# A recurrence's transposed decay products emitted ahead of the update's copy, its diagonal behind the routing, and a new order of the last steps

## The chip, the cores and the metric

One core of one Trainium2 chip. The time is device microseconds (us) of one execution of the whole program. The engines are TensorE (PE; its weight loads are listed as PEld), VectorE (DVE), ScalarE (ACT), GpSimd (POOL) and SyncE (SP, which issues most of the transfers).

## The reference, cut to what matters

Three stages follow each other. First a recurrence over 768 positions, for 4 batches and 8 heads with 48 channels:

```python
for t in range(S):
    kt, vt, rt = (k[:, :, t], v[:, :, t], r[:, :, t])
    cur = np.einsum('bhd,bhe->bhde', u[None] * kt, vt)
    y[:, :, t] = np.einsum('bhd,bhde->bhe', rt, state + cur)
    state = w[None, :, :, None] * state + np.einsum('bhd,bhe->bhde', kt, vt)
```

Then each of the 3072 tokens (384 channels) with a positive skip score goes to the one of 8 experts with the largest logit, `y = gate * relu(x @ w1[e]) @ w2[e]`, and is added to its input. Then a soft mixture: 32 slots, each a softmax-weighted sum over all tokens, go through 8 experts, and every token takes a softmax-weighted sum of the slots' results.

## The kernel before, in words

The sequence is cut into 6 chunks of 128 positions; with 4 batches that gives 24 tiles, and the recurrence is a loop (line 1012) of 24 steps `i`, one tile each, chunk after chunk. The order of the work is written out by hand: inside `manual_schedule` (line 489) each engine executes its instructions in the order in which the program emits them, and the framework only adds the waits that the tiles' reads and writes call for. Where two instructions for different engines stand in the program so decides nothing about their engines' own order, but does decide which waits for which when they touch the same tile.

A step `i` does, by helper:

- `scores(i)` (line 637): TensorE forms the masked products of r and k in PSUM tile `sc`; `later` copies one part of it out on ScalarE (line 702). Then come the two products of the tile before, `inter(i-1)` (the state's share, line 728) and `av(i-1, 0)` (first half of the scores times v, line 747), and after these the optional `between()`. Then a PSUM tile `ud` of one bank is taken (line 653). It has three column ranges: 0 to 127 for the decay products `dt_` (line 657) and, later, for their transpose `dtk`; 32 columns `rp` for the routing's places; 192 columns `up` for the update of the state. ScalarE copies `dt_` to SBUF as `dts` (line 659).
- `trx(i-2)` (line 754) transposes the finished output of two tiles before into `x`, with a ScalarE copy (line 759).
- `prep(i+1)` forms r and k scaled by the decays on VectorE (lines 626, 627) and a product on GpSimd (line 629); `prepk` a further one on GpSimd.
- `upd(i)` (line 670, steps 0 to 19) writes the update into `up`; `moved(i)` (line 686) copies it out on ScalarE; `bonus(i)` (line 673) transposes `dts` into `dtk` on TensorE. In the program `moved` stands ahead of `bonus`.
- `av(i-1, 1)` is the second half of the products of the tile before; its result is copied to `yt` by ScalarE (line 752).
- `past(i)` (line 696) masks the scores into `at` on VectorE, and `amask(i)` (line 708) overwrites their diagonal from `dtk`. `av(i, 0)` of the next step needs both.

Among these lie parts of the routing for groups of four tiles, one part in each step from 5 on. With `i - 5 = 4 rc + rb`: at rb 1 (steps 6, 10, 14, 18) `route1` forms the logits on TensorE; at rb 2 (7, 11, 15, 19; called routing steps below) `route2` transposes them, ScalarE copies them (line 855) and `route2b` finds the expert in eight small VectorE instructions (lines 870 to 889); at rb 3 (8, 12, 16, 20; placing steps below) `route3` writes the places into the `rp` columns of `ud` on TensorE, and VectorE works out the gates and places (`weave`, lines 913 to 927, of which line 924 reads `rp`) and the counts (937, 938); at rb 0 `route4` (lines 945, 946). `hots` (line 792) makes a one-hot row of 256 columns per tile. All this VectorE work is emitted behind `amask` of its step. The last 8 tiles form groups 4 (16 to 19), 5 (20, 21) and 6 (22, 23), which are routed in steps 21 to 23 and in the tail behind the loop (line 1125).

The tail finishes tiles 22 and 23, routes groups 5 and 6 (`direct` forms group 6's logits in PSUM, line 845), stores x, and forms the list `idg` of token numbers per expert: products at lines 1153 and 809, cast at line 1166. Between these TensorE also does the first third of a weighted sum over the tokens (`w1g.some(6)`, line 128). With `idg` GpSimd gathers the tokens (line 1189), and the expert stage starts (lines 1254 on); from there on TensorE is busy nearly throughout.

Of the kernel before, what the change touches and what calls it, by code (L numbers as in the profile page):

```python
# [8 lines left out]
F32 = mybir.dt.float32  # L9
# [10 lines left out]
P = 128  # L20
# [3 lines left out]
E = 8  # L24
# [447 lines left out]
def tile_main(ctx, tc, rk, kv, wu, wcat, phi, w1, w2, v1, v2, r_in, k_in, v_in, w_in, u_in, wcn, out, dbg=None, force=False):  # L472
# [199 lines left out]
    def bonus(j):  # L672
        nc.tensor.transpose(T[j]["dtk"], T[j]["dts"], ident)  # L673
# [8 lines left out]
    def moved(j):  # L682
        t = T[j]
        if j < NT - B:
            t["us"] = sp[j][1] if j < B else wk.tile([PR, 4, D], F32, tag="us", name=f"us{j}")
            nc.scalar.copy(t["us"], t["up"])
# [7 lines left out]
    def past(j):  # L694
        t = T[j]
        nc.vector.tensor_mul(t["at"][:, :, 0:4], t["sc"][:, :, 0:4], mh.rearrange("s (a o t) -> s a o t", a=1, o=1).to_broadcast([P, 2, 4, HT]))
        t["past"] = True

# [5 lines left out]
    def amask(j):  # L704
        t = T[j]
        if "past" not in t:
            past(j)
        nc.vector.copy_predicated(  # L708
            t["at"][:, :, 0:4],
            ih_i.rearrange("s (a o t) -> s a o t", a=1, o=1).to_broadcast([P, 2, 4, HT]),  # L710
            t["dtk"].rearrange("s (p o r) -> s r p o", o=1, r=32)[:, 0:2].to_broadcast([P, 2, 4, HT]),
        )
# [89 lines left out]
    def stored(j0, nb):  # L802
        nc.sync.dma_start(out=x_d.rearrange("(p j) n -> p j n", j=NT)[:, j0 : j0 + nb], in_=x[:, j0 : j0 + nb, 0:DM])
# [7 lines left out]
    lx = mk.tile([P, 4, 32], F32, name="lx")  # L811
    mcs = mk.tile([P, 5], F32, name="mcs")

    GR = [(4 * c, 4) for c in range(NC_ - 1)] + [(20, 2), (22, 2)]
# [196 lines left out]
    if True:  # L1011
        for i in range(NT):
# [4 lines left out]
            if i == 0:  # L1017
                prep(0)
                for hf in range(2):
                    r0 = 64 * hf  # L1020
                    nc.vector.tensor_copy(usel[r0 : r0 + D, :, hf : hf + 1], wt[r0 : r0 + D, 1, :].rearrange("p (a o) -> p a o", o=1))
            scores(i, lambda: route1(5) if i == 23 else None)
            if i > 1:
                trx(i - 2)
            if i == 21:
                route1(4)
            if rok and rb == 3 or i == 22:
# [5 lines left out]
            if i == 23:  # L1033
                past(23)
                mrt = ps.tile([P, 1, 32], F32, tag="t", name="mrpt")
                nc.tensor.matmul(mrt.rearrange("p o s -> p (o s)"), onesf[0:32], dgt, start=True, stop=True)
                nc.scalar.copy(lx[:, 0:1, :], mrt)
                nc.gpsimd.tensor_sub(ltm[:, 0:16, :], ltm[:, 0:16, :], lx[:, 0:1, :].to_broadcast([P, 16, 32]))
                route2(5)
# [17 lines left out]
            if i == 22:  # L1057
                c4pt = ps.tile([P, P], F32, tag="r", name="c4pt")
                nc.tensor.transpose(c4pt, c4t.rearrange("p q s -> p (q s)"), ident)
            moved(i)  # L1060
            bonus(i)
            if i > 0:
                av(i - 1, 1)
            if i in (13, 17, 21, 22):
                gathered(len(LI))
            past(i) if i < 23 else None
            if i == 22:
                nc.vector.tensor_reduce(mcs[:, 0:1], c4pt, axis=AX.X, op=ALU.max)
                dgt = rt.tile([32, 32], F32, tag="dg", bufs=1, name="dgt")
                nc.vector.tensor_scalar(dgt, ident[0:32, 0:32], mcs[0:32, 0:1], None, op0=ALU.mult)  # L1070
            amask(i)
            if i == 22:
# [4 lines left out]
            if i == 21:  # L1077
                nc.vector.tensor_reduce(cmax, cmg.rearrange("t g s -> t s g"), axis=AX.X, op=ALU.max)
                c4t = fourfold(nc, "t", rt, cmax)
                route2b(4)  # L1080
            elif rb == 0 and 1 <= rc < 4:
                route4(rc - 1)
            if rok and rb == 2 and rc < 4:
                route2b(rc)
            if rok and rb == 3:
                weave("gpgpg", g=gates(rc), p=places(rc))
                count(rc)
                tokens(rc, nc.gpsimd)
                hots(rc, (0,) if rc < 3 else (0, 1), nc.vector)
                if rc == 3:  # L1090
                    route4(3)
# [9 lines left out]
            if i % B and 9 <= i < 22:  # L1101
                hots(i // B - 2, (i % B,) if i < 20 else (2, 3), nc.vector)
            if i % B == 1 and 9 <= i < 25:
# [17 lines left out]
            if i == 6:  # L1121
                sf = rt.tile([P, E], F32, tag="sf", bufs=1, name="sf")
                nc.vector.tensor_reduce(sf, ident.rearrange("p (q r s) -> p s q r", q=4, s=E)[:, :, :, 0:2], axis=AX.XY, op=ALU.add)
                nc.vector.tensor_copy(selb, sf)
        stored(20, 2)
        inter(23)
        route2b(5)
        nc.scalar.activation(ltm[:, 0:16, :], ltm[:, 0:16, :], AF.Exp)
        av(23, 0)
        fz = T[23]["rp"][:, 3 * E : 4 * E]  # L1130
        nc.tensor.matmul(fz, ones, eb2, start=True, stop=True)
# [5 lines left out]
        hots(5, range(2), nc.gpsimd)  # L1137
        direct(6, 0)
        nc.tensor.matmul(fz, ones, fs, start=True, stop=True)
        av(23, 1)  # L1140
        scst.close()
        qst = ExitStack()
        pr = qst.enter_context(tc.tile_pool(name="pr", bufs=1, space=PSUM, side="right"))
        pc = Banks(tp=[(pr, "tp", 2)], ds=[(pr, "ds", 1)])
        trx(23, "tp", pc)
        stored(23, 1)
        direct(6, 1)
        trx(22)
        stored(22, 1)
        idp = ps.tile([P, 2, E], F32, tag="r", name="idp")  # L1150
# [507 lines left out]
```

## Time and profile before

| what | value |
|---|---|
| time, median of 3 runs | 360.18 us (360.09 to 366.7) |
| the profiled execution's own time | 361.89 us |
| its span, first to last instruction | 360.1 us |
| TensorE, busy share of the span | 91% |
| VectorE | 62% |
| ScalarE | 44% |
| GpSimd | 38% |
| mean granted TensorE clock | 0.979 of full speed |

A timeline's row is: start in us from the span's start, duration in us, engine, line, operation, output <- inputs, shapes, count; in brackets how long the engine had been idle before it and what ended that. Several equal instructions in a row are merged into one. A row of waits is: engine, tile and line that waited, what it waited for, us in total, times, the longest. Times inside the profile are those of the profiled execution; the part of its 361.89 us outside the span is 1.79 us.

### The profile page before, as it was taken

To read this page: it belongs to the slowest core of one execution; us is meant where nothing else is said; L and a number is where in the kernel's file an instruction comes from. 1 tells how busy PE (TensorE), PEld (TensorE's weight loads), DVE (VectorE), ACT (ScalarE), POOL (GpSimd) and SP (SyncE) were. 2 spreads that over 40 slices of the span, in tenths; PEclk is the share of its full clock that TensorE was granted. 3 is DMA by queue.
4 is the path that set the end of the run, shared out by engine and by line. 5 is a ranking of instruction groups with operands and counts; after the bars stand their busy time and mean duration, and the time that the engine had idled before them with its cause. 6 is when DMAs were issued, how large, how long until landed. Compare 5 with 4: busy or idle time off the path is not lost. (4 is left out here: it accounts for less than half of the span.)

```text
span 360.1 us, 10416 instructions
## 1 busy us (share of the span) xinstructions
PE 328.3 (91%) x4316; PEld 263.2 (73%) x4316; DVE 222.1 (62%) x514; ACT 160.2 (44%) x351; POOL 138.4 (38%) x175
## 2 busy tenths in 40 slices
PE   8888889888898889899999999999999999999860
PEld 3556676676767565599999999998899999733350
DVE  6455578584867853668576657567476765416660
ACT  2234444444444535246465556464465652311270
POOL 3837666575744161850525252432225202020000
PEclk9999999999999996999999999999999999999995
DMA  7975568476677962689778796978975549669586
GB/s 209 271 204 165 178 181 271 145 257 188 183 213 260 386 226 76 186 295 329 250 268 274 251 308 208 305 247 286 320 227 157 181 153 291 239 198 371 180 314 220
DMA packets 45751, 85.29 MB, mean 237 GB/s; under 512 B 3854, under 2 KB 26688, under 8 KB 45696
## 3 DMA queue, kind: packets, MB, share of 16 engines
q1 hardware_dynamic: 43040, 80.63, 68.1%
q0 software_dynamic: 2128, 3.74, 3.9%
q8 instruction: 36, 0.59, 0.7%
q10 hardware_dynamic: 528, 0.16, 0.2%
q14 instruction: 19, 0.16, 0.1%
HBM read 74.49 MB, written 10.10 MB: 235 GB/s over the span
## 5 line engine op out<-in xcount | busy, mean ns | idle before, releaser
L1254 PE MATMUL hp<-xhl,wa 128*128 128x256 f32 x192 | 48.5, 289 | 0.2 <-ACT xhl L1244 0.2
L1255 PE MATMUL hp<-xhl,wa 128*128 128x256 f32 x192 | 47.1, 282 | 0.0
L1279 PE MATMUL yp<-wb,hh 128*128 128x384 f32 x128 | 45.1, 352 | 0.0
L992 DVE TENSOR_TENSOR wa<-w,wa 128x768 fp32r<-128x768 f32 x32 | 30.5, 956 | 22.0 <-ACT wa L1004 22.0
L1281 PE MATMUL yp<-wb,hlo 128*128 128x384 f32 x128 | 42.9, 335 | 0.0
L1280 PE MATMUL yp<-wb,hh 128*128 128x384 f32 x128 | 42.9, 335 | 0.0
L629 POOL TENSOR_TENSOR pd<-rkb 112x512 f32<-112x512 f32 x24 | 30.6, 1275 | 31.2 <-PE ud L657 22.8
L708 DVE COPY_PREDICATED at<-ih,ud 128x512 f32<-128x512 int32 x24 | 17.7, 740 | 39.9 <-PE ud L673 39.6
L1189 POOL DMA_INDIRECT xg<-x_d,idg x16 | 19.2, 1202 | 53.6 <-DVE x L1287 39.4
L1309 POOL DMA_INDIRECT lt_d<-lsr,ids x16 | 17.7, 1107 | 52.4 <-ACT xhl L1244 29.8
L1254 PEld LDWEIGHTS hp<-xhl,wa 128*128 128x128 f32 x192 | 36.4, 189 | 0.5 <-ACT xhl L1244 0.5
L1255 PEld LDWEIGHTS hp<-xhl,wa 128*128 128x128 f32 x192 | 36.4, 190 | 0.0
L992 DVE TENSOR_TENSOR wb<-w,wb 128x768 fp32r<-128x768 f32 x32 | 30.5, 954 | 2.4 <-ACT wb L1004 2.3
L1264 ACT ACTIVATE hh<-hp 128x512 fp32r<-128x512 f32 x32 | 19.1, 598 | 26.0 <-PE hp L1257 26.0
L1004 ACT CAST wb<-w 128x768 fp32r<-128x768 f32 x32 | 26.8, 837 | 8.8 <-PE yp L1281 5.0
L1265 DVE SCALAR_TENSOR_TENSOR hlo<-hp,hh 128x512 fp32r<-128x512 f32 x32 | 22.0, 687 | 12.4 <-ACT hh L1264 12.4
L1257 PE MATMUL hp<-xhl,wa 128*128 128x256 f32 x192 | 28.2, 283 | 0.0
L1004 ACT CAST wa<-w 128x768 fp32r<-128x768 f32 x32 | 26.9, 840 | 0.0
L1279 PEld LDWEIGHTS yp<-wb,hh 128*128 128x128 f32 x128 | 24.1, 188 | 3.5 <-issue 3.5
L747 PE MATMUL yp<-at,kvt 64*48 64x64 f32 (+3 forms) x800 | 26.0, 245 | 0.2
L1257 PEld LDWEIGHTS hp<-xhl,wa 128*128 128x128 f32 x192 | 25.3, 192 | 0.0
L747 PEld LDWEIGHTS yp<-at,kvt 64*48 64x48 f32 (+1 forms) x800 | 20.9, 121 | 5.3 <-PE wp L498 2.2
(344 smaller groups left out, 686.0 us busy)
## 6 DMA issues: line engine op xcount, KB each, us to landing
w<-in_w_dram SPq DMA_DIRECT2D x32, 768.0 KB, 5.5
v<-in_v_dram SPq DMA_DIRECT2D x29, 768.0 KB, 6.4
rkb<-in_rk_dram SPq DMA_DIRECT2D x24, 448.0 KB, 5.2
kvt<-in_kv_dram SPq DMA_DIRECT2D x24, 384.0 KB, 3.9
x_d<-x SPq DMA_DIRECT2D x5, 768.0 KB, 8.7
out_dram<-ob SPq DMA_DIRECT2D x5, 768.0 KB, 6.1
x<-in_v_dram SPq DMA_DIRECT2D x2, 768.0 KB, 5.9
ltt<-in_v_dram SPq DMA_DIRECT2D x1, 768.0 KB, 7.2
```

Source lines behind the costliest of these rows:

```text
L629: nc.gpsimd.tensor_mul(t["pd"], rkt[:, 0], rkt[:, 1])
L747: nc.tensor.matmul(d, kvt[s0 : s0 + HT, 1, h * D : h * D + m], w, start=(c == ph == z == 0), stop=(ph == z == 1))
L992: nc.vector.tensor_sub(lv, sl, hv.bitcast(F32))
L1004: nc.scalar.copy(hv, sl)
L1189: nc.gpsimd.indirect_dma_start(out=o, out_offset=None, in_=src, in_offset=bass.IndirectOffsetOnAxis(ap=idg[:, bl, e : e + 1], axis=0), bou ...
L1254: nc.tensor.matmul(hp[:, f, :], hi[:, k, fs], xh[:, k, :], start=(k == 0 and f == 0), stop=False)
L1255: nc.tensor.matmul(hp[:, f, :], lo[:, k, fs], xh[:, k, :], start=False, stop=False)
L1257: nc.tensor.matmul(hp[:, f, :], hi[:, k, fs], xl[:, k, :], start=False, stop=(k == 2 and f == 1))
L1265: nc.vector.scalar_tensor_tensor(hlo, hp, 0.0, hh.bitcast(F32), op0=ALU.max, op1=ALU.subtract)
L1279: nc.tensor.matmul(YP[e][bl], hh[:, f, bs], hi[:, f, :], start=st, stop=False)
L1280: nc.tensor.matmul(YP[e][bl], hh[:, f, bs], lo[:, f, :], start=False, stop=False)
L1281: nc.tensor.matmul(YP[e][bl], hlo[:, f, bs], hi[:, f, :], start=False, stop=en)
```

## The change

- `bonus(i)` is emitted ahead of `moved(i)` instead of behind it.
- `amask(i)` is emitted at the end of its step, behind the routing's VectorE instructions; in step 21 behind the column maximum and ahead of `route2b(4)`. `past` is emitted at its one place in every step, 23 too.
- `hots` for group 3 (two tiles in step 20, two in step 21) go to GpSimd instead of VectorE.
- In steps 21 and 23 `route1` stands ahead of the decay products and of `trx`; in step 23 the row of maxima (`topped`: a product, a ScalarE copy, a GpSimd subtraction) stands ahead of `route1(5)` instead of behind `trx(21)`.
- In the tail the sum `fz` gets a PSUM tile of its own, tag `y`, instead of columns of `ud`; `trx(22)` moves to right behind `route3(5)`; `direct(6, 0)` goes behind `av(23, 1)`; the exponential over the first 16 tiles goes behind `trx(23)`; tiles 22 and 23 are stored in one transfer.

```diff
     def past(j):
...
-        t["past"] = True
...
     def amask(j):
         t = T[j]
-        if "past" not in t:
-            past(j)
...
+    def topped():
+        mrt = ps.tile([P, 1, 32], F32, tag="t", name="mrpt")
+        nc.tensor.matmul(mrt.rearrange("p o s -> p (o s)"), onesf[0:32], dgt, start=True, stop=True)
+        nc.scalar.copy(lx[:, 0:1, :], mrt)
+        nc.gpsimd.tensor_sub(ltm[:, 0:16, :], ltm[:, 0:16, :], lx[:, 0:1, :].to_broadcast([P, 16, 32]))
...
-            scores(i, lambda: route1(5) if i == 23 else None)
+            scores(i, lambda: (i == 23 and topped(), route1(i // 2 - 6)) if i in (21, 23) else None)
             if i > 1:
                 trx(i - 2)
-            if i == 21:
-                route1(4)
...
             if i == 23:
-                past(23)
-                mrt = ps.tile([P, 1, 32], F32, tag="t", name="mrpt")
...
                 route2(5)
...
+            bonus(i)
             moved(i)
-            bonus(i)
             if i > 0:
                 av(i - 1, 1)
...
-            past(i) if i < 23 else None
+            past(i)
...
-            amask(i)
             if i == 22:
                 weave("pgpgg", g=gates(4), p=places(4))
...
                 c4t = fourfold(nc, "t", rt, cmax)
+                amask(21)
                 route2b(4)
...
-                hots(rc, (0,) if rc < 3 else (0, 1), nc.vector)
+                hots(rc, (0,) if rc < 3 else (0, 1), nc.vector if rc < 3 else nc.gpsimd)
...
-                hots(i // B - 2, (i % B,) if i < 20 else (2, 3), nc.vector)
+                hots(i // B - 2, (i % B,) if i < 20 else (2, 3), nc.vector if i < 20 else nc.gpsimd)
...
+            if i != 21:
+                amask(i)
         stored(20, 2)
         inter(23)
         route2b(5)
-        nc.scalar.activation(ltm[:, 0:16, :], ltm[:, 0:16, :], AF.Exp)
         av(23, 0)
-        fz = T[23]["rp"][:, 3 * E : 4 * E]
+        fz = ps.tile([P, E], F32, tag="y", name="fz")
         nc.tensor.matmul(fz, ones, eb2, start=True, stop=True)
...
-        direct(6, 0)
+        trx(22)
         nc.tensor.matmul(fz, ones, fs, start=True, stop=True)
         av(23, 1)
+        direct(6, 0)
...
         trx(23, "tp", pc)
-        stored(23, 1)
+        stored(22, 2)
+        nc.scalar.activation(ltm[:, 0:16, :], ltm[:, 0:16, :], AF.Exp)
         direct(6, 1)
-        trx(22)
-        stored(22, 1)
```

## Rows read from the trace of the kernel before

**Rows 1.** Waits of TensorE, 0 to 150 us: the two largest of line 673.

```profile
PE ud L673 <- ACT us L686: 7.6, 16, 0.5
PE ud L673 <- ACT sp L686: 1.7, 4, 0.4
```

**Rows 2.** Timeline of step 15, a routing step.

```profile
88.58 0.54 PEld L670 LDWEIGHTS ud<-kvt,kt 128*64 128x64 f32 x16 [0.17 <-issue]
...
88.69 0.30 ACT L855 COPY lg<-lgp 128x168 f32<-128x168 f32 x1
...
...
89.72 0.14 PEld L673 LDWEIGHTS ud<-ident,dts 128*128 128x128 f32 x1 [0.60 <-ACT us L686]
89.73 0.33 PE L673 MATMUL ud<-ident,dts 128*128 128x128 f32 x1 [0.48 <-ACT us L686]
...
90.09 0.74 DVE L708 COPY_PREDICATED at<-ih,ud 128x512 f32<-128x512 int32 x1 [2.16 <-PE ud L673]
...
90.72 0.31 DVE L870 TENSOR_TENSOR lg<-lg,lgp 128x168 f32<-128x168 f32 x1
...
91.61 0.47 PEld L747 LDWEIGHTS yp<-at,kvt 64*48 64x48 f32 x16
...
92.77 0.68 DVE L626 TENSOR_TENSOR rks<-rkb,prt 112x512 f32<-112x512 f32 x1
```

**Rows 3.** Timeline of step 1: a product and a copy of other columns of its tile.

```profile
16.31 0.27 ACT L659 COPY dts<-ud 128x128 f32<-128x128 f32 x1 [1.35 <-PE ud L657]
...
16.67 0.64 PE L670 MATMUL ud<-kvt,kt 128*64 128x48 f32 x16 [0.43 <-issue]
```

**Rows 4.** Timeline of step 16, a placing step.

```profile
93.26 0.54 PEld L670 LDWEIGHTS ud<-kvt,kt 128*64 128x64 f32 x16
...
95.49 0.18 DVE L924 TENSOR_TENSOR r<-ud,oh 128x32 f32<-128x32 f32 x1
...
96.29 0.48 PEld L747 LDWEIGHTS yp<-at,kvt 64*48 64x48 f32 x16
...
96.64 0.68 DVE L626 TENSOR_TENSOR rks<-rkb,prt 112x512 f32<-112x512 f32 x1
```

**Rows 5.** Timeline of step 8, the first placing step.

```profile
54.73 0.18 DVE L924 TENSOR_TENSOR r<-ud,oh 128x32 f32<-128x32 f32 x1
...
56.33 0.68 DVE L626 TENSOR_TENSOR rks<-rkb,prt 112x512 f32<-112x512 f32 x1
```

**Rows 6.** Timeline of steps 21 to 23.

```profile
123.63 0.65 DVE L792 TENSOR_SCALAR hot<-ipl,sl 128x256 bf16<-128x256 f32 x2
...
127.57 3.66 POOL L792 TENSOR_SCALAR hot<-ipl,sl 128x256 bf16<-128x256 f32 x4 [3.44 <-DVE se L915]
...
130.27 0.40 PE L1036 MATMUL mrpt<-dgt,onesf 32*128 32x32 f32 x2 [0.57 <-ACT x L759]
```

**Rows 7.** Timeline of the tail.

```profile
133.46 0.17 PE L899 MATMUL ud<-eb,ones 128*128 128x16 bf16 x1 [0.82 <-ACT fs L1133]
...
135.92 0.60 PE L758 MATMUL trp<-ident,yt 112*128 112x112 f32 x4 [0.71 <-ACT yt L752]
...
137.77 0.17 DVE L875 TENSOR_REDUCE mx<-lgp 128x2 f32<-128x16 f32 x1 [3.02 <-PE lgp L845]
...
139.55 2.78 PE L128 MATMUL dpst<-x,ltt 128*32 128x385 f32 x12
...
142.26 0.29 PEld L809 LDWEIGHTS <-hot 128*128 128x128 bf16 x8 [1.24 <-issue]
...
144.76 1.48 PE L128 MATMUL dpst<-x,ltt 128*32 128x385 f32 x10
```

**Rows 8.** Busy time by stretch: us; PE, PEld, DVE, ACT, POOL; granted clock; DMA share; GB/s.

```profile
136.00:138.00 2.00, 2.00 (x15) 2.00 (x16) 0.23 (x3) 0.48 (x1) 0.27 (x1) 0.70 0.01 5
...
140.00:142.00 2.00, 2.00 (x12) 0.37 (x4) 0.69 (x4) 2.00 (x3) 0.00 (x0) 0.50 0.31 97
142.00:144.00 2.00, 2.00 (x19) 0.78 (x18) 1.20 (x4) 0.19 (x1) 0.17 (x1) 0.59 0.50 121
```

More of the change, by code (lines that the diff above doesn't have):

```diff
@@ L1033, in tile_main @@
             if i == 23:
-                past(23)
-                mrt = ps.tile([P, 1, 32], F32, tag="t", name="mrpt")
-                nc.tensor.matmul(mrt.rearrange("p o s -> p (o s)"), onesf[0:32], dgt, start=True, stop=True)
-                nc.scalar.copy(lx[:, 0:1, :], mrt)
-                nc.gpsimd.tensor_sub(ltm[:, 0:16, :], ltm[:, 0:16, :], lx[:, 0:1, :].to_broadcast([P, 16, 32]))
                 route2(5)
```

## The prediction

> **What bounds the kernel now.** I read the page first: by the table TensorE is busy for 91% of the span and no other engine above 62%. So a change pays by the idle time that it takes from TensorE, or by work that it takes off the path where TensorE waits. The second view is TensorE's list of waits over the recurrence and the tail [rows 1]. One line leads it: the transposition of the decay products, L673, waits 20 times for the copy of the update, L686, once in each of steps 0 to 19 and 9.3 us in all. The reader is to see in the timeline of one step [rows 2] why. The last weight load of the update ends at 88.58 + 0.54 = 89.12, and TensorE loads nothing until 89.72, when the copy is done: 0.60 us in which its weight path stands still. The transposition reads none of what the copy reads (`dts` lies in SBUF) and writes other columns of `ud`. That the wait is kept by tile and not by columns is seen in step 1 too: the update starts at 16.67 when the copy of the decay products, 16.31 + 0.27 = 16.58, is out of its way, though it writes other columns [rows 3]. The third view is VectorE's place in the step: the diagonal's instruction, L708, waits 2.16 us idle for the transposition, and the routing's work stands behind it [rows 2]. The last view is the tail up to the list of tokens, where TensorE waits at several places [rows 7] and has half its clock for a stretch [rows 8].
>
> **The order of transposition and copy.** With the transposition first in the program, TensorE has no wait left between update and transposition: the transposition needs only `dts`, long copied. Its weight load then starts at 89.12 or a little later. From above the gain is the 0.60 of the weight path, from below the 0.48 that the matmul's own row shows [rows 2]; nothing excludes a few hundredths lost at the hand-over, so I take 0.56, and 0.51 for the first four steps, whose matmul rows are 0.05 shorter (1.7 / 4 against 7.6 / 16 [rows 1]). The copy in turn now waits for the transposition. It starts some 0.37 later against the update's end, but has room: ScalarE's next copy, that of the second products, comes behind these products anyway, and GpSimd needs the update a chunk later. What is late next? `av(i, 0)` of the next step, if the diagonal isn't ready.
>
> **The diagonal behind the routing.** In a step with little routing VectorE does that work in the 2 us in which it waited, and the diagonal follows the transposition as before; that hides it. In two kinds of steps it doesn't.
>
> Routing steps (7, 11, 15, 19), by step 15 [rows 2]: the copied logits are there at 88.69 + 0.30 = 88.99, the eight instructions and the one-hot row take from 90.72 to the next instruction's start at 92.77, so 2.05. The diagonal would start at 88.99 + 0.03 + 2.05 = 91.07 (0.03 is the hand-over as it was before L708: 90.09 less 90.06) and be ready at 91.07 + 0.74 + 0.03 = 91.84. Before, the products' load began at 91.61. So this step loses 0.23 instead of gaining 0.56. Step 7 has no one-hot row (92.77 - 92.51 = 0.26) and comes out at -0.03, about nothing.
>
> Placing steps (8, 12, 16, 20), by step 16 [rows 4]: L924 reads the places in `ud`. By the rule of rows 3 it now waits for the transposition, which is emitted ahead of it and writes that tile. The update's load comes at 93.26 + 0.23, its end 0.54 later at 94.03; the diagonal used to start 0.37 behind the transposition's load (90.09 - 89.72 [rows 2]), so L924 starts at 94.40. From there to the next VectorE instruction were 96.64 - 95.49 = 1.15; the diagonal starts at 95.55, and the products at 95.55 + 0.77 = 96.32 against 96.29 before. The pair 15 and 16 costs 0.03 and gains nothing, 11 and 12 the same. In step 8 the chain is 56.33 - 54.73 = 1.60 long [rows 5], 0.45 more, and the pair 7 and 8 costs 0.03 - 0.26 + 0.45 = 0.22.
>
> The Trainium skill, PSUM — Partial Sum Buffer, section on bank collisions, says that two engines must be kept apart by bank and quadrant of partitions and not by address. Rows 3 agree, and it speaks against this part. If columns counted, L924 would not wait, the placing steps would each gain some 0.5, and the whole would be 1.6 us better; by the rule it is as worked out above.
>
> So of steps 0 to 18, thirteen gain in full: 4 x 0.51 + 9 x 0.56 = 7.08. Less 0.22 + 0.03 + 0.03 that is 6.8 us at the start of step 19.
>
> **The last steps and the tail.** I look for what can leave TensorE's path up to the list of tokens. Two one-hot rows on VectorE, 0.65 [rows 6], go to GpSimd, where one takes 3.66 / 4 = 0.92 and the engine had been idle for 3.44: hidden, as their reader is a step away. The wait of the product of maxima, 0.57 [rows 6], goes, since it no longer stands behind the copy of a transposed tile. In the tail the wait for `fs`, 0.82, goes as the sum gets its own bank; the wait for the last copy of yt, 0.71, is filled with `direct(6, 0)`; and one set of transpositions, 0.60 by the row of its twin, moves from the stretch behind into one where TensorE waited [rows 7]. All five make 3.35, the upper end. Against it stand step 19 (0.23) and step 20, whose diagonal comes behind weave, counts and `route4`: about 0.5, between nothing and the 0.60 that a routing step's swing less its own gain can reach. That leaves 2.6. The lower end counts the tail's two waits alone, 0.82 + 0.71, less those 0.7: 0.8. I take 2.6, since VectorE's chain is what the removed waits ended in. Stores and gather: the x of tiles 22 and 23 now leaves in one transfer on SP's queue, behind the copy of the later; both copies are earlier than before, and the gather still waits for the list. The exponential moves behind that copy on ScalarE and is read only by the weighted sum, some microseconds on.
>
> The sum is 6.8 + 2.6 = 9.4 us. The expert stage behind is bound by TensorE and moves as a whole. The sum is made in a span of 360.1 us, 361.89 with the 1.79 around it; the median of the runs is 360.18, so the time would be 350.8 us.
>
> **The clock.** TensorE's clock was at half (1.2 GHz) from inside the stretch 136 to 138 to inside 142 to 144: 0.6 x 2 + 4 + 0.82 x 2 = 6.8 us [rows 8], behind the tail's idle time. The weighted sum took 0.23 per product in that stretch (2.78 / 12) and 0.15 at full clock (1.48 / 10) [rows 7]. I assume that the fall comes again about there, since the new tail still waits for group 5's experts and then does only small products.
>
> **The rivals.**
> - *The clock holds.* Less idle time stands ahead of the place of the fall. Then the first twelve products take 1.4 us less (139.55 to 142.26 is 2.7, half of it), and the list comes that much sooner: 360.18 - 10.8 = 349.4. For it: two of the waits ahead go. Against: the small products stay.
> - *The diagonal comes later than worked out.* If readers of `ud` on two engines are also kept apart, L924 waits for the copy of the update as well, some 0.35 more in each of steps 8, 12 and 16, and if the transposition's gain is only the 0.48 of its row, thirteen steps lose 0.08 more: 1.05 + 1.0. With 2 us for the tail instead of 2.6 that is 6.7, so 353.5. For it: VectorE has no slack in the pairs. Against: nothing in the rows shows such a wait.
> - *The transposition still waits.* If its wait came from something else than the order in the program, the 7.08 are gone and the diagonals are late for nothing: some 0.8 us in each of three pairs. Against that stand the tail's 2.6: 360. Against it: the wait ends with that copy in 20 of 20 steps.
> - *Slower: the clock falls inside the recurrence.* New waits of TensorE for the diagonal come in groups: steps 7 and 8, 11 and 12, 15 and 16, 19 and 20, and 22. If the clock fell there as in the tail, each fall would cost half of 6.8, or 3.4 us. Three falls eat the gain (10.2 of 9.4), and five make it 360.18 - 9.4 + 17 = 367.8. Against it: every step had an idle 0.6 before with the mean clock at 0.979, and the new waits are no longer than those that go. The Trainium skill, TensorE: Matmul & The Clock Gate, section on oscillation, says that idle gaps between bursts of matmuls throttle the engine again; the half clock behind the tail's waits agrees, and no row shows it in the recurrence.
>
> **How the numbers follow.** Forecast 350.8: 0.45 (own range 349.3 to 352.3). Clock holds, 349.4: 0.25. Diagonal late, 353.5: 0.21. Transposition still waits, 360: 0.06. Clock falls, 367.8: 0.03. A measurement of this kernel can tell about 2% from no change, so faster is below 353.0: nearly all of the first two and a third of the third, held back a little as my durations come from one execution: 0.73. Slower, above 367.4: 0.03. Within: 0.24. The range runs from 347.0, where the tail gives its whole 3.35 (0.75 more), the 0.60 is reached in each of thirteen steps (0.7) and the clock holds, with 1 us over for what the rows of one execution leave open, to 354.5, which takes in the late diagonal and a tail with 1 us less.
>
> **What would show it.** Right: L673 has no wait for L686 in the list of waits, and 20 steps' L673 load follows L670's at once; L686 now waits for L673. L747 waits for L708 by 0.5 to 1 us in steps 7, 8, 11, 12, 15, 16, 19 and 20, and in no other up to there. L924 starts right behind the transposition. Step 19 starts some 6.8 us earlier, the list (L1166) some 9.4. The prediction is wrong if waits for L708 show in steps with little routing, if L673 waits for another engine, if the stretch from step 19 to the list isn't some 2.6 us shorter, or if the granted clock is below 1.00 between 10 and 130 us.

## The result, and the profile after

The changed kernel takes 356.97 us (median of 20 runs, 353.27 to 362.22); the kernel before, run beside it on the same chip, takes 361.85 (20 runs). The ratio is 0.985, with an interval of 0.982 to 0.987: a gain of 1.5%, within the 2%. The forecast was a gain of 9.4 us; about half of it came. A median is of all executions; a ratio and its interval leave out those more than 1.5% above the fastest of their kernel. The granted clock differs between executions of one program (0.964 to 0.987 here) and the time mostly goes with it, 353.27 us at 0.987 and 356.98 at 0.976. The rows below are of one execution each, that of the changed kernel one of 355.71 us at 0.985; those of e4_swap_only, e5_wok_late and e9_mixed, further down, took 364.11, 361.53 and 355.44 us, more than these kernels' medians.

The page's table and clock of the changed kernel:

```profile
span 354.0 us, 10396 instructions
## 1 busy us (share of the span) xinstructions
PE 326.0 (92%) x4316; PEld 261.7 (74%) x4316; DVE 230.9 (65%) x510; ACT 160.8 (45%) x351; POOL 141.7 (40%) x179
...
PEclk9999999999999999999999999999999999999985
```

VectorE's share of the span is up from 62% (222.1 us), though it executes four instructions fewer. TensorE's waits, 0 to 150 us, answer to [rows 1]:

```profile
PE yp L744 <- DVE at L705: 6.8, 9, 1.4
...
PE ud L910 <- DVE oh L892: 0.4, 1, 0.4
```

The 9.3 us of L673 are gone from the list; the products (L744, before L747) wait for VectorE's diagonal (L705, before L708) instead, nine times, 6.8 us. VectorE's own waits in the same stretch, first the diagonal of the kernel before, then the changed kernel:

```profile
DVE at L708 <- PE ud L673: 39.6, 20, 3.6
```

```profile
DVE at L705 <- ACT us L686: 8.7, 5, 2.1
DVE at L705 <- ACT sp L686: 8.0, 4, 3.0
DVE at L705 <- PE ud L673: 4.1, 2, 2.5
...
DVE r L927 <- ACT us L686: 3.4, 3, 1.1
```

The reader is to see the name L686: before, the diagonal waited 20 times for the transposition; now it waits for that twice and nine times for the copy of the update, which only reads the same tile. The places' product (L927, before L924) waits for that copy too. The third reading is the timeline of steps 11 and 12, a routing and a placing step, which answer to [rows 2] and [rows 4] (L789 is the one-hot row, before L792):

```profile
66.52 0.33 DVE L873 TENSOR_TENSOR lg<-lg,lgp 128x168 f32<-128x168 f32 x1 [0.94 <-ACT lg L858]
...
68.22 0.19 DVE L892 SCALAR_TENSOR_TENSOR oh<-lgp,m 128x32 bf16<-128x32 f32 x1
...
68.33 0.70 DVE L789 TENSOR_SCALAR hot<-ipl,sl 128x256 bf16<-128x256 f32 x1
68.35 0.52 POOL L680 TENSOR_TENSOR tmp<-sp,pt 112x192 f32<-112x192 f32 x1
...
68.95 0.71 DVE L705 COPY_PREDICATED at<-ih,ud 128x512 f32<-128x512 int32 x1
...
69.71 0.55 PE L744 MATMUL yp<-at,kvt 64*48 64x128 f32 x16 [0.85 <-DVE at L705]
...
71.88 0.33 PE L673 MATMUL ud<-ident,dts 128*128 128x128 f32 x1
...
72.30 0.32 ACT L686 COPY us<-ud 112x192 f32<-112x192 f32 x1 [0.63 <-PE ud L673]
...
72.65 0.19 DVE L927 TENSOR_TENSOR r<-ud,oh 128x32 f32<-128x32 f32 x1 [1.13 <-ACT us L686]
...
73.52 0.70 DVE L789 TENSOR_SCALAR hot<-ipl,sl 128x256 bf16<-128x256 f32 x1
73.55 0.52 POOL L680 TENSOR_TENSOR tmp<-sp,pt 112x192 f32<-112x192 f32 x1
...
74.14 0.71 DVE L705 COPY_PREDICATED at<-ih,ud 128x512 f32<-128x512 int32 x1
...
74.90 0.55 PE L744 MATMUL yp<-at,kvt 64*48 64x128 f32 x16 [0.84 <-DVE at L705]
```

Two things stand here that the forecast did not have (the first was a rival's). The places' product starts when the copy of the update ends (72.30 + 0.32 = 72.62), not behind the transposition. And the one-hot row takes 0.70 where it took about 0.34, and is done (0.70 on from 73.52 is 74.22) soon after the GpSimd multiply that began beside it (74.07). Between 50 and 103 us there are eleven such rows, each 0.69 us or longer, and each ends 0.15 or 0.16 us behind the end of a GpSimd instruction. VectorE's one-hot rows by form, 0 to 135 us, first of the changed kernel, then of the kernel before, with busy us and mean ns of one:

```profile
L789 DVE TENSOR_SCALAR hot<-ipl,sl 128x256 bf16<-128x256 f32 x14 | 10.4, 748 | 0.0
```

```profile
L792 DVE TENSOR_SCALAR hot<-ipl,sl 128x256 bf16<-128x256 f32 x16 | 5.4, 345 | 0.0
```

It is the same instruction at more than twice the time. The worst case of this kind is in step 4, where constants are made; first the cast of the kernel before, then the timeline of VectorE and GpSimd in the changed kernel:

```profile
35.04 0.21 DVE L1114 CAST tf<-tj_i 128x48 f32<-128x48 int32 x1
```

```profile
30.38 1.27 POOL L629 TENSOR_TENSOR pd<-rkb 112x512 f32<-112x512 f32 x1 [0.58 <-PE ud L657]
...
30.70 1.96 DVE L1110 CAST tf<-tj_i 128x48 f32<-128x48 int32 x1
...
31.61 1.00 POOL L635 TENSOR_TENSOR kt<-kvt,pktok 128x384 f32<-128x384 f32 x1
...
33.60 0.71 DVE L705 COPY_PREDICATED at<-ih,ud 128x512 f32<-128x512 int32 x1
```

A cast of 48 elements per partition, 0.21 us before, lasts until both GpSimd instructions are over (32.61), and step 5 is 0.55 us longer than before.

The time from the start of one step's scores to the next, taken from the timelines (all in us; the last column sums steps 3 to 18). The products that need the diagonal of a step belong to the next one, so a late diagonal in step 4 shows in step 5, one in steps 7 and 8 in 8 and 9:

```
                  step 5   8+9   12+13   16+17   19 to 22   3 to 18
before             4.44   9.16    9.60    9.49      20.31     81.56
after              4.99  10.15   10.53   10.53      18.67     80.51
e1_front           4.06  10.93    8.80    8.82      20.17     81.19
e2_copy_first      4.52  10.24   10.53   10.52      18.69     84.68
e4_swap_only       4.07  10.92    8.80    8.81      23.98     80.54
e6_fill_behind     4.06   8.98    9.31    9.31      18.58     76.17
e7_wok_psum        4.06   8.95    8.81    8.80      20.17     75.76
e8_own_bank        4.03   8.10    9.27    9.26      21.06     75.40
e11_hots_behind    4.99   9.64    9.30    9.31      18.58     78.52
e12_const_behind   4.06   9.58   10.52   10.50      18.66     78.94
```

Step 19, whose first products need the diagonal of step 18, a step with little routing, went from 4.92 to 4.37, a gain of 0.55. The scores of step 19 start 2.1 us earlier (105.82 to 103.70), the list of tokens 7.2 us earlier (142.68 to 135.50). Of these 7.2 us the span keeps 6.1 (360.1 to 354.0): from the list to the end it takes 218.5 us instead of 217.4. A wait of TensorE for a transfer, which the kernel before does not have there, makes 0.6 of that; where the rest lies was not looked for.

```profile
PE sop L232 <- DMA v<-in_v_dram: 0.6, 1, 0.6
```

The tail shows neither of the two waits of [rows 7] (0.82 and 0.71), and its clock is not that of [rows 8]; busy time of the changed kernel by stretch, PE alone, granted clock in the third column from the end:

```profile
130.00:136.00 6.00, 5.81 (x100) 1.00 0.21 70
136.00:143.00 7.00, 5.78 (x51) 1.00 0.66 196
```

### The profile page after: what moved, and what is told of

The parts are those of the page before. It is cut to its first block, busy times and chain, and to the rows that moved or that the text cites. A ratio compares the mean times of both kernels' runs of the same rounds, so it can differ in the third digit from the quotient of the medians.

```text
span 354.0 us, 10396 instructions
## 1 busy us (share of the span) xinstructions
PE 326.0 (92%) x4316; PEld 261.7 (74%) x4316; DVE 230.9 (65%) x510; ACT 160.8 (45%) x351; POOL 141.7 (40%) x179
## 5 line engine op out<-in xcount | busy, mean ns | idle before, releaser
L744 PE MATMUL yp<-at,kvt 64*48 64x64 f32 (+3 forms) x800 | 26.4, 248 | 7.2 <-DVE at L705 6.8
L744 PEld LDWEIGHTS yp<-at,kvt 64*48 64x48 f32 (+1 forms) x800 | 20.0, 120 | 15.0 <-DVE at L705 9.6
L705 DVE COPY_PREDICATED at<-ih,ud 128x512 f32<-128x512 int32 x24 | 17.4, 726 | 20.8 <-ACT us L686 8.7
L1261 ACT ACTIVATE hh<-hp 128x512 fp32r<-128x512 f32 x32 | 19.1, 598 | 26.0 <-PE hp L1254 26.0
```

Source lines behind the costliest of these rows:

```text
L744: nc.tensor.matmul(d, kvt[s0 : s0 + HT, 1, h * D : h * D + m], w, start=(c == ph == z == 0), stop=(ph == z == 1))
```

## The experiments

Theory 1 was that the late place of the diagonal ate the gain, theory 2 that VectorE's small instructions stand still beside GpSimd's, theory 3 that reads of one PSUM tile by two engines keep the program's order.

**The parts alone.** Four kernels take the change apart.

```diff
 e1_front: the changed kernel, amask(i) right behind past(i) again
 e2_copy_first: the changed kernel, moved(i) ahead of bonus(i) again
 e3_tail_only: both of these
 e4_swap_only: the kernel before, with
+            bonus(i)
             moved(i)
-            bonus(i)
```

e1_front was expected so: 

> The changed kernel with one part undone: VectorE's diagonal stands again behind the causal products, ahead of the routing's work; the transposition ahead of the copy and the new tail stay. Theory 1 (the late place of the diagonal is what ate the gain): no step waits for the diagonal, all 20 steps with an update gain 0.50 to 0.56, some 10.5 us at step 20, and with the tail's 3.4 the time is about 13 to 14 us under the kernel before: 346 to 348. Rival (the diagonal is late wherever it stands, since it waits for the update's copy, and the routing behind it then waits too): not better than the changed kernel, 355 to 358.

Measured: 357.99 us, ratio 0.989 (0.985 to 0.993). The time is at the upper end of the rival's, but not for its reason: TensorE waits nowhere for the diagonal. Steps 12, 13, 16 and 17 did gain (17.6 us in all, against 21.1 in the changed kernel and 19.1 before), but step 9 took 6.42 and step 10 8.17. TensorE's waits of e1_front from 50 to 60 us, and VectorE's and GpSimd's timeline of its step 8:

```profile
PE sc L647 <- DVE at L696: 2.7, 2, 2.5
```

```profile
53.88 1.27 POOL L629 TENSOR_TENSOR pd<-rkb 112x512 f32<-112x512 f32 x1 [0.16 <-PE ud L657]
53.98 2.13 DVE L1092 SCALAR_TENSOR_TENSOR wok<-wt,wok 112x4 f32<-112x4 f32 x1
55.10 0.99 POOL L635 TENSOR_TENSOR kt<-kvt,pktok 128x384 f32<-128x384 f32 x1
...
56.23 0.68 DVE L626 TENSOR_TENSOR rks<-rkb,prt 112x512 f32<-112x512 f32 x1
```

Four elements per partition take 2.13 us: the instruction, the second of three that test the weights `wt` (tile `wok`), starts just behind the start of pd and ends with kt (56.09). Everything on VectorE is that much later, and the scores wait 2.5 us. Then the clock falls; e1_front by stretch (PE; granted clock third from the end):

```profile
48.00:58.00 10.00, 7.40 (x200) 0.97 0.84 257
58.00:64.00 6.00, 5.84 (x80) 0.50 0.45 137
64.00:68.00 4.00, 3.96 (x102) 0.98 0.13 18
```

Six microseconds at 1.2 GHz, right behind the stop of 2.5. So this one instruction cost 2.0 us in step 9 and 2.3 in step 10 (6.42 and 8.17 against 4.44 and 5.83 in e7_wok_psum below, which differs in its operand alone).

e2_copy_first was expected so: 

> The changed kernel with the other part undone: the copy of the update is again ahead of the transposition; the diagonal stays behind the routing and the new tail stays. Theory 1: the plain steps gain nothing; in the steps where the changed kernel lost (5, 9, 12, 13, 16, 17: 0.4 to 1.07 each, 3.6 in all) the same is lost, against the tail's 3.4: about 360, no difference. Rival (the losses belong to the transposition's new place, not to the diagonal's): only the tail's gain is left and no step is slower, 356 to 357.

Measured: 360.0 us, ratio 0.995 (0.993 to 0.997). As theory 1 and 2 have it: steps 12 and 13 take 10.53, as in the changed kernel to the hundredth, with the copy ahead of the transposition. The loss of these steps belongs to the diagonal's place. Step 5 does not fit: one of the constants takes 2.08 us there too, but the step takes 4.52, not 4.99, and loses only 0.08 against before.

e3_tail_only was expected so: 

> Both parts of the recurrence undone (copy ahead of the transposition, diagonal in its old place); the new order of the last steps and of the tail is all that is left of the change. Theory: steps 0 to 20 are as before; from the scores of step 23 to the list 3.4 us less with the clock at full speed there, 2.0 with a fall as before (it was worth 1.4 of the 3.4): 356 to 358.5. Rival (the tail gained only because the work ahead of it came early): no difference, 359 to 360.5.

Measured: 362.24 us median of 12, ratio 0.995 (0.991 to 1.000); so the median lies outside the expectation and above the rival's range; the profiled execution, 357.07, lies inside. From the scores of step 23 to the list it takes 13.68 against 16.55 before and 13.13 in the changed kernel, with the clock at full speed. The rest of its executions, but for two, ran at a granted clock of 0.969 to 0.975 and took 361.14 us or more; where in the span the clock fell in them no trace shows.

e4_swap_only was expected so: 

> The kernel before with one thing new: the transposition is emitted ahead of the update's copy. Theory 1: 20 steps gain 0.50 to 0.56, the diagonal follows the update's copy instead of the transposition, some 0.3 later, and the products, which came 0.78 behind it, still don't wait: 349 to 350.5, with the tail's clock falling as before. Rival (the diagonal, held by the copy, is late for the products in the shorter steps): 20 waits of 0.1 to 0.5, 352 to 358.

Measured: 361.82 us, ratio 0.998 (0.995 to 1.002). That is 11 us over the first theory's range, and the rival's reason isn't there either: no wait for the diagonal. But step 9 takes 6.42 and step 10 8.38 as in e1_front, with the same 2.13 us of L1096 in its step 8, and the clock falls there and again at 117 to 125, behind a stop of 1.77 us that the profile does not name.

**The stretched instruction.** e5 to e7 test theory 2.

```diff
 e5_wok_late: e1_front, the three instructions on wt from step 8 to behind tensor_copy(idg, idp)
 e7_wok_psum: e1_front, with
-                wok = rt.tile([PR, 4], F32, tag="wok", name="wok")
+                wok = RT[0]["lgp"][0:PR, 0, 114:118]
 e6_fill_behind: the changed kernel, wok as in e5, and
                 count(rc)
                 tokens(rc, nc.gpsimd)
-                hots(...)
...
+            if i != 21:
+                amask(i)
+            if rok and rb == 3:
+                hots(...)
...
-            if i != 21:
-                amask(i)
```

e5_wok_late was expected so: 

> The changed kernel with the diagonal back in its old place (as in e1_front) and, beside that, the three small instructions that test the weights (wok, 112x4) moved from step 8 to behind the list of tokens. Theory 2 (VectorE's instructions that read and write only SBUF stand still while a GpSimd instruction runs, here for two in a row, 2.13 us for 4 elements): the wait of the scores for the causal product in step 9, 2.5 us, goes, and so does the fall of the clock behind it: steps 9 and 10 take 4.1 to 4.4 and 5.5 to 5.7 us instead of 6.42 and 8.17, and the time is 4 to 5 us under e1_front's 358: 353 to 354. Rival (the long instruction only showed a VectorE that is late anyway): the next instruction stands still in its place, no difference from e1_front.

Measured: 355.36 us, ratio 0.985 (0.979 to 0.991). Steps 9 and 10 take 3.98 and 6.10: the stop and the fall behind it are gone, though step 10 stays above the 5.5 to 5.7 expected. In time only 2.6 of the 4 to 5 came, and the interval overlaps that of e1_front, so here the steps decide and not the time. The profiled execution, the longest of the six, shows a fall of the clock in steps 2 and 3 (at the stop shown for e9_mixed below), which e1_front had too.

e7_wok_psum was expected so: 

> e1_front with one operand in another memory: the first wok lies in spare columns of a PSUM tile instead of in SBUF, so that the instruction that took 2.13 us reads one operand from SBUF and one from PSUM; its place, its size and what GpSimd does beside it are the same. Theory 2: it takes some 0.2 us and the time falls as in e5_wok_late, 353 to 354. Rival (it waits for VectorE's or GpSimd's order, whatever the memories): 2 us as before, 358.

Measured: the instruction's row in e7_wok_psum, by line, and two rows of the timeline beside it:

```profile
L1092 DVE SCALAR_TENSOR_TENSOR wok<-wt,lgp 112x4 f32<-112x4 f32 x1 | 0.2, 157 | 0.0
```

```profile
51.65 1.27 POOL L629 TENSOR_TENSOR pd<-rkb 112x512 f32<-112x512 f32 x1 [0.15 <-PE ud L657]
...
52.02 0.68 DVE L626 TENSOR_TENSOR rks<-rkb,prt 112x512 f32<-112x512 f32 x1
```

157 ns instead of 2130, at the same place beside pd (it ran at 51.75, pd from 51.65 to 52.92). So this instruction stands still when both its operands lie in SBUF, and does not with one in PSUM. L626 agrees: one of its operands, `prt`, lies in PSUM, and with 512 elements per partition it takes 0.68 us inside pd, as it does where GpSimd is idle (0.66 to 0.68). Steps 9 and 10 take 4.44 and 5.83. The time is no clean answer, 359.28 us median with a ratio of 0.986 (0.974 to 0.998): its runs go from 353.5 at a clock of 0.976 to 362.05 at 0.962.

e6_fill_behind was expected so: 

> The changed kernel with the diagonal still behind the routing, the places and the counts, but ahead of the one-hot rows (hot), of the constants of steps 3 to 6 and with wok moved to behind the list. Theory 2: what made the diagonal late was for the larger part these fillers, which GpSimd's instructions stretched from 0.34 to 0.70 to 1.16 and from 0.2 to 1.96: step 5 takes 4.4 instead of 4.99, step 9 4.5 to 4.9 instead of 5.55, steps 12, 13, 16 and 17 together 1.2 to 2.0 less; the time is 3 to 4.5 us under the changed kernel's 357.0: 352.5 to 354. Rival (the routing's own chain behind the copy is what is late): steps 12, 13, 16 and 17 keep their 5.2 to 5.3, under 1.5 us gained.

Measured: 351.18 us, ratio 0.973 (0.967 to 0.979), faster than both kernels and over 1 us better than expected. The diagonal still stands behind the routing; only the fillers have moved, that is what nothing in the step waits for: the one-hot rows, the constants and wok. TensorE's waits of e6_fill_behind, 0 to 150 us, and its one-hot rows by form:

```profile
PE yp L744 <- DVE at L705: 2.3, 8, 0.6
```

```profile
L789 DVE TENSOR_SCALAR hot<-ipl,sl 128x256 bf16<-128x256 f32 x14 | 6.0, 438 | 0.0
```

The wait for the diagonal falls from 6.8 to 2.3 us, and steps 3 to 18 take 76.17, which is 5.4 under before.

**e6_fill_behind taken apart.** Two kernels move one kind of filler each: e11 only the hots, e12 only the constants and wok.

e11_hots_behind was expected so: 

> e6_fill_behind taken apart, first half: of the changed kernel only VectorE's one-hot rows (hot, steps 8 to 19) are moved, from ahead of the diagonal to behind it; the constants of steps 3 to 6 and the three instructions on the weights stay ahead of it. If the hots' stretch beside GpSimd is what the routing and placing steps lost: steps 12, 13, 16 and 17 take 4.6 to 4.75 each as in e6_fill_behind (5.2 to 5.3 in the changed kernel), step 9 4.9 to 5.1, and step 5 keeps its 4.99; 3.0 to 3.5 us under the changed kernel: 353 to 354.5. If not, these steps stay at 5.2.

Measured: 351.82 us, ratio 0.974 (0.969 to 0.978). Step 5 keeps its 4.99, step 9 takes 5.04, and steps 12, 13, 16 and 17 take 4.59, 4.71, 4.59 and 4.72, as expected; the time is better than the 353 to 354.5 expected.

e12_const_behind was expected so: 

> e6_fill_behind taken apart, second half: of the changed kernel only the constants of steps 3 to 6 are moved behind the diagonal, and the three instructions on the weights to behind the list; the hots stay ahead of the diagonal. Step 5 takes 4.06 instead of 4.99, step 9 some 0.5 less than 5.55, and steps 12, 13, 16 and 17 keep their 5.2 to 5.3; 1.3 to 2.0 us under the changed kernel: 355 to 356. The two halves together should make the 5.5 to 6 us between the changed kernel and e6_fill_behind.

Measured: 353.74 us, ratio 0.980 (0.976 to 0.984). Step 5 takes 4.06, step 9 4.99, and the four steps keep their 5.2 to 5.3, as expected; the time is better than expected by 1 to 2 us. Step by step the halves make the whole: 0.93 in step 5, 0.51 + 0.56 in step 9 (e6_fill_behind: 1.17), 2.45 in the four. The times add up only within their intervals: by the ratios the halves save 1.1% and 0.5% against the changed kernel, the whole 1.2%.

**The readers of one tile.**

```diff
 e8_own_bank: e5_wok_late, and in bonus(j)
+        T[j]["dtk"] = ps.tile([P, P], F32, tag="t", name=f"dtk{j}")
         nc.tensor.transpose(T[j]["dtk"], T[j]["dts"], ident)
```

e8_own_bank was expected so: 

> e5_wok_late with the transposed decays in a PSUM tile of their own (that of the transposed outputs) instead of in the tile with the update and the places. Theory 3 (reads of one PSUM tile by two engines are kept in the program's order): VectorE's diagonal starts behind the transposition, about 0.3 earlier in its step, and not behind the copy of the update. As nothing waits for the diagonal in e5_wok_late, the time is the same, 353 to 354; the four gathers of the one-hot rows now wait for it, up to 0.7 each: 353 to 356. Rival (the wait for the copy was only that both follow the transposition): the diagonal starts as far behind the transposition as before.

Measured: 354.37 us, ratio 0.981 (0.973 to 0.989). VectorE's waits and the timeline of step 10 of e8_own_bank, then step 13 of e6_fill_behind, one with little routing:

```profile
DVE at L706 <- PE dtk L674: 30.6, 15, 3.1
```

```profile
57.67 0.33 PE L674 MATMUL dtk<-ident,dts 128*128 128x128 f32 x1
57.85 0.32 ACT L687 COPY us<-ud 112x192 f32<-112x192 f32 x1
...
58.03 0.74 DVE L706 COPY_PREDICATED at<-ih,dtk 128x512 f32<-128x512 int32 x1 [1.78 <-PE dtk L674]
```

```profile
72.68 0.33 PE L673 MATMUL ud<-ident,dts 128*128 128x128 f32 x1
73.10 0.32 ACT L686 COPY us<-ud 112x192 f32<-112x192 f32 x1 [0.43 <-PE ud L673]
73.45 0.74 DVE L705 COPY_PREDICATED at<-ih,ud 128x512 f32<-128x512 int32 x1
```

The diagonal waits for the transposition again, starts 0.36 behind its start (0.77 in e6_fill_behind) and no longer behind the copy, which ends at 58.17. Theory 3 holds, and the time is inside the expectation. The gathers of steps 13, 17, 21 and 22 wait 3.3 us for it in turn, so what the order of the readers costs in the placing steps is not isolated in time.

**Two more versions.** e9_mixed is e6_fill_behind with the diagonal of steps 0 to 16 ahead of the routing and that of 17 to 23 behind it; e10_swap_wok is e4_swap_only with wok behind the list.

e9_mixed was expected so: 

> e6_fill_behind with the diagonal of steps 0 to 16 in its old place, ahead of the routing, and only from step 17 on behind it. In the profiles so far steps 12 to 17 take 27.4 us in all with the diagonal ahead (e7_wok_psum) and 28.4 behind the routing (e6_fill_behind), and steps 18 to 22 the other way round: 26.6 against 24.0. If these add up: 1.0 us under e6_fill_behind, 350 to 350.5. Rival (the earlier the products, the sooner TensorE meets another stop, as loads or its own instructions): no better than e6_fill_behind, 351 to 353.

Measured: 351.95 us median, ratio 0.968 (0.963 to 0.973), the lowest ratio of all, yet not told apart from e6_fill_behind; the median is in the rival's 351 to 353. Steps 12, 13, 16 and 17 take 17.6 as expected, but step 18 takes 6.73 where e6_fill_behind has 5.43. Its profiled execution shows the other stop, in step 2 (timeline of PE, then stretches as above):

```profile
19.54 1.44 PE L498 MATMUL wp<-ones 128*128 128x512 bf16 x3 [2.12 <-issue]
```

```profile
18.00:20.00 2.00, 0.46 (x2) 0.73 1.03 268
20.00:28.00 8.00, 7.94 (x107) 0.50 0.61 153
```

TensorE stands for 2.12 us ahead of three filler products, for nothing that the profile names, with the DMA engines full (share 1.03), and then has half its clock for some 10 us. In the kernels before and after 1.02 and 1.09 us of idle time stand at the same place, without a fall. But in e12_const_behind it is 2.14 us, and the clock stays at full speed behind it:

```profile
19.32 0.81 PE L498 MATMUL wp<-ones 128*128 128x512 bf16 x3 [2.14 <-issue]
```

```profile
20.00:28.00 8.00, 7.87 (x206) 1.00 0.71 199
```

e10_swap_wok was expected so: 

> The kernel before with the transposition ahead of the copy (as e4_swap_only) and the three small instructions on the weights moved behind the list; the diagonal, the last steps and the tail are those of before. Theories 1 and 2 together: what e4_swap_only lost in steps 9 and 10 (2.1 and 2.9 with the clock's fall) goes; the 20 steps give 7 to 9 us at step 20 by the first term of the prediction, and the time is 352 to 354, with the tail's clock as before. Rival (a TensorE without the stops of 0.5 meets others and the clock falls for these): 357 to 361, as e4_swap_only.

Measured: 357.2 us, ratio 0.986 (0.981 to 0.990). By the time it is the rival's, by the steps the theories': step 19 starts at 99.06, 6.8 earlier than before (1.3 of which lie ahead of step 0), the list 6.5 earlier. The tail's clock falls as in [rows 8], and steps 14 and 18 lose 1.0 and 1.4 against e6_fill_behind to waits that the profile names "issue" or the causal product.

## Why the prediction was wrong

**The order of transposition and copy: right.** Steps 7, 11 and 15, each behind a step with little routing, gained 0.54 to 0.55 where 0.56 was worked out. L673 waits for nothing, L686 waits for it. In e10_swap_wok, with the diagonal in its old place, steps 0 to 18 take 5.5 us less than before.

**The diagonal's cost: wrong, by 5.0 of the 6.8 us.** From step 0 to step 19 the measured gain is 1.84 (97.12 less 95.28). The difference stands in these places:

- *"In a step with little routing VectorE does that work in the 2 us in which it waited ... that hides it."* Step 4 has none of the routing's work but seven small instructions for constants, priced at nothing. Beside GpSimd's instructions three of them take 1.96 + 0.50 + 0.44 = 2.9 us (0.63 before), TensorE waits 0.82 us for the diagonal, and step 5 loses 0.55 instead of gaining 0.56: 1.1 us. e12_const_behind gives 0.93 of it back.
- *The chains, 2.05 behind the copied logits and 1.15 behind L924, at their durations of before.* They take 68.95 - 66.52 = 2.43 and 74.14 - 72.65 = 1.49; both differences are the one-hot row's 0.70 in place of 0.34. In the kernel before, behind the diagonal, the row began while GpSimd was idle or within 0.2 us of the end of its instruction (step 12: at 72.02, GpSimd idle from 70.88 to 72.18); ahead of it, it meets GpSimd's multiply of the state. e11_hots_behind, which takes the whole row out of the chain, gives 1.2 us back in each of two pairs of steps.
- *"By the rule of rows 3 it now waits for the transposition": too weak a rule.* The row showed a write kept from a read. The runs show that a read by VectorE is kept behind a read by ScalarE as well: L927 starts at 72.65, where the transposition alone would let it at 71.88 + 0.37 = 72.25. That is 0.40 a placing step, close to the rival's 0.35.

Together the pairs came out at -0.99, -0.93 and -1.04 instead of -0.22, -0.03 and -0.03, which is 2.7. Step 0 lost 0.12 instead of gaining 0.51; it lies in the start, which differs from profile to profile (4.41 or 4.42 in six of the other kernels). The last 0.5 is in smaller pieces, the largest 0.19 in step 10. Of the prediction's own signs, the waits for the diagonal came in all eight places that it names, 0.25 to 1.41 us, and in one more, that behind step 4, which it had called a sign of being wrong.

The Trainium skill, SBUF — State Buffer, section on SBUF's two separate sides, states the mechanism: VectorE and GpSimd share a pair of ports, which one of them holds for a whole instruction while the other is blocked; on VectorE's side this concerns instructions in a two-port mode, and those with two SBUF inputs against a GpSimd one that reads SBUF. e7_wok_psum agrees (2130 ns with two SBUF operands, 157 with one in PSUM); in which mode the cast and the one-hot row ran, no row tells. The runs show more than the page: a waiting VectorE instruction can miss its turn between two GpSimd instructions that follow each other (2.13 and 1.96 us across pd and kt). It need not: in e6_fill_behind a one-hot row from 55.09 ends at 55.69, just behind GpSimd's addition (55.54) and ahead of the end of the multiply that follows it (56.06).

**The last steps and the tail: right in kind, too small.** From step 19 to the list 5.06 us came (36.86 to 31.80), where 2.6 was forecast and 4.0 with the clock held. Steps 19 to 22 gave 1.64, for which the prediction had a loss of 0.7 and parts of its five items; they give it with the diagonal behind the routing (18.7 in e2_copy_first) and not with it ahead (20.3 in e3_tail_only). From the scores of step 23 on it was 3.42 with the clock at full speed. In e6_fill_behind, where the clock is at half for some 3.4 us from 127.5 to 131, it was 2.1. So the rival that the clock holds came true in this execution, as one case among several. This part gave 2.5 us more than forecast and so hides part of the miss in the recurrence.

**"The expert stage behind ... moves as a whole": wrong by 1.1 us.** Of the 7.2 us at the list (0.3 of them from the start) 6.1 reach the end of the span. Between the two profiled executions that makes 6.2 us of time; the medians are 4.9 apart, as the changed kernel's median is 1.3 above its profiled execution, at a lower granted clock.

**The rivals.** The late diagonal came true in its mechanism, but that is 0.40 in each of three placing steps, 1.2 of the 5.0 us; the stretched instructions, which make most of the rest, stand in no rival. It was priced at 353.5 and 356.97 came. The slower rival, a fall of the clock inside the recurrence, did not come in the profiled execution (1.00 from 10 to 130 us) but did in e1_front and e4_swap_only, after stops of 2.5 us: step 10 takes 2.3 and 2.6 us more there than in e7_wok_psum, less than the 3.4 worked out. The waits for the diagonal, up to 1.4 us, brought none in the recurrence in any profile.

## What to carry to other kernels

A move on an engine's queue changes what runs beside the moved instructions, and their durations with it: before a row's time is used at a new place, look what GpSimd does there, and where the operands of VectorE's instruction lie. For an instruction with two operands in SBUF, moving one to PSUM took it out of GpSimd's way here; so does a place where GpSimd is idle. On a queue that feeds the bound engine, what nobody waits for goes behind what is waited for: with its fillers behind the diagonal the same change is worth 2.7% instead of 1.5%.

## What the runs showed of the hardware that was not expected

- Some VectorE instructions with only SBUF operands lasted until the GpSimd instructions beside them were over: one on 4 elements per partition 2.13 us instead of 0.16, a cast of 48 elements 1.96 instead of 0.21, a one-hot row 0.69 to 1.16 instead of 0.34.
- Reads of one PSUM tile by ScalarE and VectorE ran one after the other, in the program's order, though nothing writes between them; with a second tile the later reader started 0.4 us sooner. Whether the chip needs that or only the program's waits make it so, no row tells.
- Inside the recurrence TensorE's clock went to half behind stops of 1.8 to 2.5 us (e1_front, e4_swap_only, e5_wok_late, e9_mixed); behind stops of 1.4 (the changed kernel), 1.5 (e4_swap_only, in step 2) and 2.14 us (e12_const_behind) it stayed at full speed, so the length of a stop alone does not tell. The times of one program, 353.27 to 358.49 at a clock of 0.987 to 0.972, say that it falls in some executions and not in others.
